# Larger first-stage and inverse units on three PSUM banks in a fused FFT filter and hardswish MLP

## The chip, the core and the metric

The kernel runs on one core of one Trainium2 chip. The metric is the device time of one launch in microseconds (us). The core's engines work side by side and each takes its own instructions in order: TensorE (PE: matmuls; PEld: its weight loads), VectorE (DVE), ScalarE (ACT), GpSimd (POOL) and SyncE (SP), whose queue here only issues DMAs.

## The reference

Eight sequences of 3008 rows and 256 columns are filtered along the rows in the frequency domain. The result, 24064 rows, goes through an MLP with a hardswish.

```python
X = np.fft.rfft(x, axis=1)                 # x: (8, 3008, 256)
Y = X * (filt_r + 1j * filt_i)[None]       # filter: (1505, 256)
y = np.fft.irfft(Y, n=3008, axis=1)
x = y.reshape(8 * 3008, 256)
h = x @ w_in                               # (256, 2048)
g = h * np.clip(h + 3.0, 0.0, 6.0) / 6.0
out = g @ w_out                            # (2048, 256)
```

All is in float32. A matmul in float32 leaves two records in the profile, one for each of its two passes.

## The kernel before

**The transform.** A sequence ("image" in what follows) has 3008 = 47 x 64 rows. The transform over the 47 is the first stage, the one over the 64 the second, and the inverse goes back the same way:

- The first stage works on 32 pairs of columns (HC). `a_unit(b, c)` (L439) takes four of them, in eight matmuls of 47 rows of contraction, 64 output rows and 256 columns. The contraction uses half of the array's rows and the output half of its columns, so four matmuls can be in the array at a time. The two halves h of the rows write into two PSUM banks from the pool psF, which has two buffers. ScalarE copies the first bank into the tile t1 (L449). `a_sums` (L453) lets VectorE subtract and add the second (L459, L460). `z_store` (L462) writes the four parts of the tile to the DRAM tensor z_tmp, by DMAs on POOL's queue.
- `x_load(b, c)` (L381) loads four pairs of columns into one of three buffers of the tile xs, with four DMAs on SP's queue. `t2_load` reads z_tmp back for the second stage.
- `b_unit` (L485) is the second stage, two y tiles at a time for images 2 to 7. `f_unit` (L505) multiplies with the filter on VectorE (L514 to L516), reading PSUM. `y_unit` (L519) combines the products into a y tile (L525, L526).
- `bi_unit(b, i)` (L530) is the first inverse stage: two y tiles, four matmuls of 64 rows, 64 output rows and 512 columns into two banks of psF. ScalarE copies both banks (L540) into the tile t3, of which there is one buffer (T3B). `g_store` (L550) writes it to g_tmp by DMAs on POOL's queue.
- `t4_load`, `n_unit` (L633) and `n_five` (L618) do the last inverse stage into the ring xn. Once a block of the ring is full, POOL forms the sums that the MLP needs (`t_sums`, L676, L683).

**The MLP.** There are 47 blocks of 512 rows (block 0 is done in a plain way). Each has eight steps p, one for each 256 of the 2048 hidden columns. Both products are done by Strassen's scheme, with seven smaller products in place of eight. One step on TensorE:

1. `up_1` (L689): A11 into the bank al, S1 and A12 into the bank be.
2. The place for early units, `do(0)`.
3. Down product 1 of the step before (L763).
4. `up_2` (L702): S2 into al, S4 into be. Afterwards VectorE reads be in `up_2b` (L713), which gives the first half of h.
5. Down products 2 and 4; `up_3`: S3 into al, which VectorE reads in L718; down products 5 and 6.
6. `up_4` (L720): ScalarE's relu of the first half; then the place `do(1)`.
7. VectorE's `hswish(k, p, 0)` (L737); `up_5` (L724): A22 into al, whose result ScalarE copies and puts through relu.
8. Down products 7 and 3, then the place `do(2)`.

al and be are one bank each (pool psU, one buffer), and four banks (psO) collect the down products. [...]

VectorE begins the next step with `g_sums` (L740): `hswish(k, p, 1)` (L737) and three sums (L744, L745, L747), on which down products 2 to 7 rest. L713, L718 and `hswish(k, p, 0)` follow.

At the end of a block, in the step p = 0 of the next one, `out_2` (L829) follows `hswish(k, p, 0)` on VectorE, and `out_3` (L834) follows the last down products 7 and 3. In p = 1, `out_4` (L838, L839) comes before L713 and `out_5` (L843) before `hswish(k, p, 0)`.

**The order.** It is written out by hand (`manual_schedule`). The dictionary `plan` holds, for each step of the whole run, what is put at its three places. Units of TensorE are in EARLY (L893) and go to place 0. What is not in EARLY, as `a_sums`, `f_unit`, `y_unit` and the DMAs, goes to place 2; place 1 holds only `w_scale`, early in the run. `places(n)` (L1058) gives the steps for image n. It counts them from 8 x `first[n]`, the first step of the block with which the image begins. Steps are named by this distance here: step -48 is 48 before it and so a step p = 0. For images 2 to 7 first-stage units stand at -54, -52, -49, -47, -45, -43, -42 and -41, inverse units at -32, -26, -23, -16, -10 and -7. One image takes about 47 steps of the MLP, so the stages of the next image lie under the MLP of the one before.

Of the kernel before, what the change touches and what calls it, by code (L numbers as in the profile page):

```python
# [10 lines left out]
FP32 = mybir.dt.float32  # L11
I32 = mybir.dt.int32
AXT = mybir.ActivationFunctionType
ALU = mybir.AluOpType
# [13 lines left out]
NA = 47  # L28
NC = 64
KH = 24  # L30
X0, XR = 16, 112
NF = N // 2 + 1
P = 128
D = 256
# [3 lines left out]
HC = NC // 2  # L38
XC = 4
NB = HC // XC  # L40
TC = 4
NT = KH // TC
TB = 3
# [138 lines left out]
def kernel(  # L182
# [64 lines left out]
    st = {}  # L247
# [130 lines left out]
    G11, G3, G1, G2, G4, G12, G22 = range(7)  # L378


    def x_load(b, c):  # L381
        t = xs[:, (b * NB + c) % 3, :, :]
        rows = x[b].rearrange("(a c) d -> a c d", c=NC)
        for h in range(2):
            for r, n in ((0, 32), (32, NA - 32)):
                nc.sync.dma_start(t[h * 64 + r:h * 64 + r + n, :, :], rows[r:r + n, ds(h * HC + c * XC, XC), :])

# [65 lines left out]
    def a_sums(b, c):  # L453
        t, ps = st["t1", b, c]
        if b == 1:
            if c >= NB - 2:
                nc.vector.tensor_copy(out=t[:, :, 1, :], in_=ps)
            return
        nc.vector.tensor_tensor(out=t[:, :, 1, :], in0=t[:, :, 0, :], in1=ps, op=ALU.subtract)  # L459
        nc.vector.tensor_tensor(out=t[:, :, 0, :], in0=t[:, :, 0, :], in1=ps, op=ALU.add)  # L460

    def z_store(b, c, q=nc.gpsimd):  # L462
        t = st.pop(("t1", b, c))[0]
# [66 lines left out]
    def bi_unit(b, i, ps=None):  # L530
        ys = [st.pop(("y", b, i + v)) for v in range(2)]
        ps = ps or [psF.tile([P, 2, D], FP32, name="psf", tag="f") for ri in range(2)]
        for v, ri in ((0, 0), (1, 0), (0, 1), (1, 1)):

            products = isinstance(ys[v], tuple)
            w, y = (wi[:, 1 + ri, :], ys[v][ri]) if products else (wi[ts(ri, 64), 0 if b else 3, :], ys[v][ts(ri, 64)])
            nc.tensor.matmul(ps[ri][ts(v, 64)], w, y, start=True, stop=True)  # L537
        t = (t3p if b or i & 2 else t1p).tile([P, 2, 2, D], FP32, name="t3" if b or i & 2 else "t1")
        for ri in range(2):
            nc.scalar.activation(out=t[:, ri, :, :], in_=ps[ri], func=AXT.Copy)  # L540
        st["t3", b, i] = t

    def g0_first(i):
        t = st["t3", 0, i]
# [348 lines left out]
    EARLY = (a_unit, b_unit, bi_unit, n_unit, n_five)  # L893

    def at(step, fn, *a):
        plan.setdefault((step, 0 if fn in EARLY else 1 if fn == w_scale else 2), []).append((fn, a))

    with tc.manual_schedule():

# [155 lines left out]

        def places(n):  # L1058
            if n == 1:
                return (list(range(2, NB + 2)), [12, 13, 15, 18, 19, 20, 22, 23, 26, 27, 28, 30],  # L1060
                        [14, 15, 16, 19, 21, 22, 24, 25, 27, 29, 30, 31], [16, 21, 24, 29, 31, 32])
            k = first[n] * NP
            a_at = [k - 7 * NP + i for i in (2, 4, 7, 9, 11, 13, 14, 15)]
            f_at, y_at, bi_at = ([k - (5 - 2 * r) * NP + i for r in range(2) for i in p]
                                 for p in ((2, 3, 6, 7, 12, 13), (4, 5, 10, 11, 14, 15), (8, 14, 17)))
            return a_at, f_at, y_at, bi_at

        at(n_at[TAIL - 2] + 1, lambda: nc.sync.dma_start(edge, wai_d[:, ds(NW + ND, ND)]))
# [2 lines left out]
        for n in range(1, B):  # L1071
            a_at, f_at, y_at, bi_at = places(n)
            for c, s in enumerate(a_at):
                at(s, a_unit, n, c)
                at(s, a_sums, n, c)
                at(s, z_store, n, c, nc.sync if n == 1 else nc.gpsimd)
                if c >= 3:
                    at(max(a_at[c - 3], s - 6), x_load, n, c)
                elif n > 1:
                    at(max(prev[c + NB - 3], s - 6), x_load, n, c)  # L1080
            for c in range(NT):
                s = f_at[2 * (c - TB) + (n == 1)] + 1 if c >= TB else a_at[-1] + 1
                at(s, t2_load, n, c)
                s = f_at[2 * (c - FB) + 1] + 1 if c >= FB else a_at[-1 if n > 1 else 3] + 1
                at(s, table_load, n, c)
            for i in range(NU):
                if i % 2 == 0 or n == 1:
                    at(f_at[i], b_unit, n, i)
                if i % 2 == 0:
                    at(bi_at[i // 2], bi_unit, n, i)  # L1090
                    at(bi_at[i // 2], g_store, n, i)
                at(y_at[i], y_unit, n, i)
            for i in range(NU):
                at(f_at[i], f_unit, n, i)
            prev = a_at
# [4 lines left out]
        for i in range(len(items) + 1):  # L1100
            up = i < len(items)
            k, p = items[min(i, len(items) - 1)]
            dn = i > 0
            kd, pd = items[i - 1]
            def do(place):
                for fn, a in plan.get((i, place), ()):
                    fn(*a)

            if k == 0:
                plain_up(p)  # L1110
                do(0)
# [12 lines left out]
            dn = dn and kd > 0  # L1124
            if dn:
                g_sums(kd, pd)
                down(kd, pd, 1)
            if up:
                up_2(k, p)
            if dn and pd == 0 and kd > 1:  # L1130
                out_4(kd - 1)
            if up:
                up_2b(k, p)
            if dn:
                down(kd, pd, 2, 4)
                if pd == NP - 1:
                    out_1(kd)
            if up:
                up_3(k, p)
            if dn:  # L1140
                down(kd, pd, 5, 6)
            if up:
                up_4(k, p)
                do(1)
            if ends:
                out_1(k)
            if last_plain:
                plain_down(pd, (0,))
            if dn and pd == 0 and kd > 1:
                out_5(kd - 1)  # L1150
            if up:
                hswish(k, p, 0)
            if up:
                up_5(k, p)
            if last_plain:
                plain_down(pd, (1,))
                plain_out()
            if dn:
                if pd == NP - 1 or ends:
# [35 lines left out]
```

## Time and profile before

| what | value |
|---|---|
| time, median of 3 runs | 2660.61 us (2660.59 to 2660.66) |
| the profiled execution | 2658.29 us |
| its span, first to last instruction | 2656.3 us |
| granted TensorE clock | 1.000 |
| first-stage matmuls L446, 896 records | 61.7 us busy, 389 ns mean |
| inverse matmuls L537 from y, 336 records | 51.2 us busy, 615 ns mean |
| ACT copy of a bank, 128x512, L449 | 600 ns mean |
| VectorE sums, 128x512, L459 and L460 | 681 and 687 ns mean |
| POOL's z stores L467, issue | 504 ns mean |
| POOL's g stores L553, issue | 591 ns mean |

The busy time of a row is the union of its instructions' times, so matmuls that run side by side count once. The mean is that of one record. In a timeline, each line has the start in us from the span's start, the time that the merged instructions took, engine, line, operation, what is written and read, shape and count.

### The profile page before, as it was taken

Reading aid. Unit: us, or ns where it says so; the run is one execution under the profiler, and the core shown is the slowest. Engines: PE = TensorE matmul, PEld = TensorE weight load, DVE = VectorE, ACT = ScalarE, POOL = GpSimd, SP = SyncE. Lnnn points to the kernel's source line nnn. Section 1 sums busy time; section 2 is a strip of 40 time slices with the busy share of each in tenths; the row PEclk is TensorE's granted clock in tenths of the full one; section 3 lists DMA queues with packets and bytes.
Section 4 is the critical chain, followed back from the end, with each engine's and each line's share of the span. In section 5 each row is a group of like instructions: output and inputs, shape, how many; then the busy total and the mean of one; then the engine's idle time right before and its main releaser. Section 6 shows DMA issues by size and latency. Waiting matters only on the chain.

```text
span 2656.3 us, 54240 instructions
## 1 busy us (share of the span) xinstructions
PE 2640.7 (99%) x21584; PEld 2316.5 (87%) x21584; DVE 2053.4 (77%) x3488; ACT 1318.7 (50%) x2688; POOL 495.6 (19%) x731
## 2 busy tenths in 40 slices
PE   9999999999999999999999999999999999999999
PEld 6688888888888888888888888888888888899998
DVE  7878868887688877888768887788877878766666
ACT  4554454555545554454544545545455454554554
POOL 2242021110311103111031210311113120111110
PEclk9999999999999999999999999999999999999999
DMA  9732233112241122411323113231122421110000
GB/s 251 216 91 74 68 96 105 56 36 81 79 109 56 36 83 76 109 56 37 87 72 109 56 40 85 70 109 56 49 77 70 109 59 50 42 43 21 20 20 24
DMA packets 134818, 198.24 MB, mean 75 GB/s; under 512 B 23146, under 2 KB 99016, under 8 KB 134374
## 3 DMA queue, kind: packets, MB, share of 16 engines
q1 hardware_dynamic: 117037, 150.12, 19.8%
q0 software_dynamic: 16960, 44.16, 6.3%
q8 instruction: 170, 2.79, 0.4%
q14 instruction: 82, 0.67, 0.1%
q10 hardware_dynamic: 569, 0.50, 0.1%
HBM read 122.43 MB, written 83.98 MB: 78 GB/s over the span
## 4 chain that ended last, share of the span: by engine, by line
PE 95%; DVE 2%; DMA 1%; issue 0%; ACT 0%; SPq 0%; POOL 0%; POOLq 0%; DVEq 0%; ACTq 0%
PE po L763 43%; PE al L687 24%; PE be L687 17%; PE psf L446 2%; PE psn L627 2%; PE psf L537 2%; PE psf L493 1%; PE po L806 1%; PE al L795 0%; PE be L795 0%; DMA w_all<-in_x_dram 0%; DVE g L737 0%; PE po L502 0%; DMA out_dram<-o 0%; PE psn L638 0%
## 5 line engine op out<-in xcount | busy, mean ns | idle before, releaser
L763 PEld LDWEIGHTS po<-w_all,g 128*128 128x128 f32 x10276 | 1362.1, 191 | 153.3 <-issue 44.5
L763 PE MATMUL po<-w_all,g 128*128 128x128 f32 x10276 | 1402.3, 276 | 0.1
L732 ACT ACTIVATE r<-h,half_c 128x512 f32<-128x512 f32 x736 | 532.9, 724 | 356.4 <-DVE h L713 344.5
L737 DVE SCALAR_TENSOR_TENSOR g<-r,h 128x512 f32<-128x512 f32 x736 | 531.3, 722 | 215.2 <-ACT r L732 203.2
L687 PE MATMUL al<-xt,w_all 128*128 128x256 f32 x2208 | 659.6, 381 | 0.1
L687 PE MATMUL be<-xt,w_all 128*128 128x256 f32 x1472 | 437.8, 379 | 0.0
L713 DVE TENSOR_TENSOR h<-be,s 128x512 f32<-128x512 f32 x368 | 253.8, 690 | 157.2 <-PE be L687 151.3
L687 PEld LDWEIGHTS al<-xt,w_all 128*128 128x128 f32 x2208 | 335.4, 192 | 1.0 <-issue 0.5
L687 PEld LDWEIGHTS be<-xt,w_all 128*128 128x128 f32 x1472 | 279.7, 190 | 37.9
L727 ACT ACTIVATE h<-al 128x256 f32<-128x256 f32 x368 | 141.7, 385 | 319.8 <-PE al L687 319.7
L718 DVE TENSOR_TENSOR h<-al,s 128x256 f32<-128x256 f32 x368 | 155.9, 424 | 149.6 <-PE al L687 148.5
L745 DVE TENSOR_TENSOR g<-g 128x512 f32<-128x512 f32 x367 | 261.7, 713 | 12.6
L708 ACT ACTIVATE s<-al 128x256 f32<-128x256 f32 x368 | 141.8, 385 | 194.6 <-PE al L687 191.2
L553 POOL DMA_DIRECT2D g_tmp<-t x96 | 55.4, 591 | 938.2 <-ACT t L540 926.2
L699 ACT ACTIVATE s<-be 128x256 f32<-128x256 f32 x368 | 141.7, 385 | 175.9 <-PE be L687 175.9
L687 PE MATMUL al<-xn,w_all 128*128 128x256 f32 x736 | 222.5, 384 | 1.4 <-DVE h L718 1.3
L687 PE MATMUL be<-xn,w_all 128*128 128x256 f32 x736 | 218.9, 379 | 0.0
L683 POOL TENSOR_TENSOR xt<-xn 128x256 f32<-128x256 f32 x184 | 136.7, 761 | 433.7 <-ACT xn L609 399.6
L744 DVE TENSOR_TENSOR g<-g 128x256 f32<-128x256 f32 x367 | 172.7, 471 | 12.5
L698 ACT ACTIVATE s<-al 128x256 f32<-128x256 f32 x368 | 141.8, 385 | 67.8 <-PE al L687 67.8
L747 DVE TENSOR_TENSOR g<-g 128x256 f32<-128x256 f32 x367 | 160.1, 436 | 12.5
L467 POOL DMA_DIRECT2D z_tmp<-t x192 | 95.3, 504 | 364.9 <-DVE t L460 347.5
(152 smaller groups left out, 1846.7 us busy)
## 6 DMA issues: line engine op xcount, KB each, us to landing
g_tmp<-t POOLq DMA_DIRECT2D x96, 256.0 KB, 3.7
t<-g_tmp SPq DMA_DIRECT2D x184, 120.0 KB
t<-z_tmp SPq DMA_DIRECT2D x42, 512.0 KB
z_tmp<-t POOLq DMA_DIRECT2D x192, 96.0 KB, 2.5
xs<-in_x_dram SPq DMA_DIRECT2D x112, 128.0 KB
o_tmp<-o SPq DMA_DIRECT2D x46, 256.0 KB
ft<-in_filt_r_dram SPq DMA_DIRECT2D x168, 64.0 KB
ft<-in_filt_i_dram SPq DMA_DIRECT2D x168, 64.0 KB
```

What stands on the lines that cost most here:

```text
L687: nc.tensor.matmul(ps, w_in[p][:, w, :], x, start=start, stop=stop, skip_group_check=True)
L698: nc.scalar.activation(out=s[:, 0, :], in_=al, func=AXT.Copy)
L699: nc.scalar.activation(out=s5, in_=be[:, 1, :], func=AXT.Copy)
L708: nc.scalar.activation(out=s[:, 1, :], in_=al, func=AXT.Copy)
L713: nc.vector.tensor_tensor(out=st["h"][0].rearrange("p (a n) -> p a n", a=2), in0=be, in1=s, op=ALU.add)
L718: nc.vector.tensor_tensor(out=st["h"][1][:, 256:512], in0=al, in1=s5, op=ALU.add)
L732: nc.scalar.activation(out=r, in_=st["h"][i], func=AXT.Relu, bias=half_c, scale=1.0 / 6.0)
L737: nc.vector.scalar_tensor_tensor(out=st["g", k, p][:, o:o + 2, :].rearrange("p a n -> p (a n)"), in0=st["r", i], scalar=1.0, in1=st["h"][i ...
L744: v.tensor_tensor(out=g[:, G1, :], in0=g[:, G3, :], in1=g[:, G22, :], op=ALU.add)
L745: v.tensor_tensor(out=g[:, G3:G2 + 1:2, :], in0=g[:, G3:G1 + 1, :], in1=g[:, G11:G11 + 1, :].broadcast_to([P, 2, 256]), op=ALU.subtract)
L747: v.tensor_tensor(out=g[:, G4, :], in0=g[:, G12, :], in1=g[:, G2, :], op=ALU.subtract)
L763: nc.tensor.matmul(st["po", k][bank][:, part, u, :], g[:, a, ts(u, P)], w_out[p][:, w, :], start=(p == 0 and n in OPENS and u == 0), stop= ...
```

## The change

The change touches images 2 to 7; image 1 keeps its units.

- `a6_unit`, `a6_sums` and `z6_store` take the place of `a_unit`, `a_sums` and `z_store`. A unit has six pairs of columns in 12 matmuls, three rounds of four. Per image there are five of these and one of two pairs of columns (SIX). The third bank is be, the one that `up_1` and `up_2` use. In round 1 the half h = 1 writes into be, in round 3 the half h = 0. ScalarE copies 64 columns of be after round 1 and the other 192 at the end.
- `bi3_unit` and `g3_store` take the place of `bi_unit` and `g_store`: three y tiles, again 12 matmuls of 256 columns on two banks of psF and on be. VectorE copies be in two parts, ScalarE one bank in the unit and the other in `bi3_copies`, after `up_5`.
- Both units go to place 1, between `up_4` and `up_5`, so just ahead of A22.
- The tile t3 gets three parts and serves both kinds of unit; there is still one buffer. xs serves as two buffers of six pairs of columns.
- First-stage units now stand at -52, -50, -48, -46, -43 and -41, inverse units at -30, -23, -14 and -7. The y units move from (4, 5, 10, 11, 14, 15) to (4, 5, 8, 10, 14, 15) in each half of the image, so from -30 and -29 to -32 and -30, and from -14 and -13 to -16 and -14.

```diff
+SIX = tuple(range(0, HC, 6))
...
+    def x_at(b, c):
+        if b == 1:
+            return xs[:, (b * NB + c) % 3, :, :], c * XC, XC
+        t = xs.rearrange("p i j d -> p (i j) d")
+        return t[:, ds((b * len(SIX) + c) % 2 * 6, 6), :], SIX[c], min(6, HC - SIX[c])
+
     def x_load(b, c):
-        t = xs[:, (b * NB + c) % 3, :, :]
+        t, c0, n_ = x_at(b, c)
...
+    def a6_unit(b, c):
+        xc, c0, n = x_at(b, c)
+        n //= 2
+        t = t3p.tile([P, 3, 2, D], FP32, name="t3")
+        banks = [psF.tile([P, 512], FP32, name="psf", tag="f") for h in range(2)]
+        be = psU.tile([P, 512], FP32, name="be") if n == 3 else None
+        for r in range(n):
+            for g in range(2):
+                for h in range(2):
+                    j, ps, o = (2, be, h) if r == 2 - 2 * h and n == 3 else (r - h if n == 3 else 0,) + (banks[h], r - h if n == 3 else 0)
+                    q = g * n + j
+                    nc.tensor.matmul(ps[ts(g, 64), ts(o, D)], wa[ds(h * 64, NA), ds((c0 + q) * 2 * KH, 64)],
+                                     xc[ds(h * 64, NA), q, :], start=True, stop=True)
+            if n == 3 and r == 0:
+                nc.scalar.activation(out=t[:, 2, 1, 0:64], in_=be[:, D:D + 64], func=AXT.Copy)
+        m = min(n, 2)
+        two = [ps[:, 0:m * D].rearrange("p (j d) -> p j d", d=D) for ps in banks]
+        nc.scalar.activation(out=t[:, 0:m, 0, :], in_=two[0], func=AXT.Copy)
+        if n == 3:
+                nc.scalar.activation(out=t[:, 2, 1, 64:D], in_=be[:, D + 64:], func=AXT.Copy)
+        st["t1", b, c] = t, be, two[1], n
+
+    def a6_sums(b, c):
+        t, be, ps, n = st["t1", b, c]
+        v, m = nc.vector, min(n, 2)
+        if n == 3:
+            v.tensor_tensor(out=t[:, 2, 0, :], in0=be[:, 0:D], in1=t[:, 2, 1, :], op=ALU.add)
+            v.tensor_tensor(out=t[:, 2, 1, :], in0=be[:, 0:D], in1=t[:, 2, 1, :], op=ALU.subtract)
+        v.tensor_tensor(out=t[:, 0:m, 1, :], in0=t[:, 0:m, 0, :], in1=ps, op=ALU.subtract)
+        v.tensor_tensor(out=t[:, 0:m, 0, :], in0=t[:, 0:m, 0, :], in1=ps, op=ALU.add)
...
+    def bi3_unit(b, i):
+        ys = [st.pop(("y", b, i + v)) for v in range(3)]
+        c = psU.tile([P, 512], FP32, name="be")
+        banks = [psF.tile([P, 512], FP32, name="psf", tag="f") for ri in range(2)]
+        t = t3p.tile([P, 3, 2, D], FP32, name="t3")
+        to = [t[:, q, :, :].rearrange("p u d -> p (u d)") for q in range(3)]
+        for r in range(3):
+            for v in range(2):
+                for ri in range(2):
+                    x, u, ps, o = (2, v, c, ri) if r == 2 * ri else (v, r - 1 + ri, banks[ri], r - 1 + ri)
+                    nc.tensor.matmul(ps[ts(v, 64), ts(o, D)], wi[ts(ri, 64), 0, :], ys[x][ts(ri, 64), u, :], start=True, stop=True)
+            if r == 0:
+                nc.vector.tensor_copy(out=to[2][:, 0:64], in_=c[:, 0:64])
+        nc.scalar.activation(out=to[1], in_=banks[1], func=AXT.Copy)
+        nc.vector.tensor_copy(out=to[2][:, 64:512], in_=c[:, 64:512])
+        st["t3", b, i] = t
+        st["bi3"] = to[0], banks[0]
+
+    def bi3_copies():
+        if "bi3" in st:
+            to, ps = st.pop("bi3")
+            nc.scalar.activation(out=to, in_=ps, func=AXT.Copy)
...
     def at(step, fn, *a):
-        plan.setdefault((step, 0 if fn in EARLY else 1 if fn == w_scale else 2), []).append((fn, a))
+        plan.setdefault((step, 0 if fn in EARLY else 1 if fn in (w_scale, bi3_unit, a6_unit) else 2), []).append((fn, a))
...
+        A_AT = (4, 6, 8, 10, 13, 15)
...
-            a_at = [k - 7 * NP + i for i in (2, 4, 7, 9, 11, 13, 14, 15)]
+            a_at = [k - 7 * NP + i for i in A_AT]
             f_at, y_at, bi_at = ([k - (5 - 2 * r) * NP + i for r in range(2) for i in p]
-                                 for p in ((2, 3, 6, 7, 12, 13), (4, 5, 10, 11, 14, 15), (8, 14, 17)))
+                                 for p in ((2, 3, 6, 7, 12, 13), (4, 5, 8, 10, 14, 15), (10, 17)))
...
             if up:
                 up_5(k, p)
+            bi3_copies()
```

`z6_store` and `g3_store` issue four DMAs for each unit on POOL's queue, as `z_store` did; `g_store` issued two.

More of the change, by code (lines that the diff above doesn't have):

```diff
@@ L385, in x_load @@
             for r, n in ((0, 32), (32, NA - 32)):
-                nc.sync.dma_start(t[h * 64 + r:h * 64 + r + n, :, :], rows[r:r + n, ds(h * HC + c * XC, XC), :])
+                nc.sync.dma_start(t[h * 64 + r:h * 64 + r + n, 0:n_, :], rows[r:r + n, ds(h * HC + c0, n_), :])
     def x0_at(o, n):
@@ L460, in a_sums, with z6_store @@
         nc.vector.tensor_tensor(out=t[:, :, 0, :], in0=t[:, :, 0, :], in1=ps, op=ALU.add)
+    def a6_unit(b, c):
[27 more added lines that the diff above has]
+        v.tensor_tensor(out=t[:, 0:m, 0, :], in0=t[:, 0:m, 0, :], in1=ps, op=ALU.add)
+    def z6_store(b, c):
+        t, _, _, n = st.pop(("t1", b, c))
+        for g in range(2):
+            for ri in range(2):
+                p0 = g * 64 + ri * KH
+                nc.gpsimd.dma_start(z_d[b, :, ri, ds(SIX[c] + n * g, n), :, :].rearrange("k j s d -> k (j s d)"),
+                                    t[p0:p0 + KH, 0:n, :, :].rearrange("p j s d -> p (j s d)"))
     def z_store(b, c, q=nc.gpsimd):
@@ L537, in bi_unit @@
             nc.tensor.matmul(ps[ri][ts(v, 64)], w, y, start=True, stop=True)
-        t = (t3p if b or i & 2 else t1p).tile([P, 2, 2, D], FP32, name="t3" if b or i & 2 else "t1")
+        t = t3p.tile([P, 3, 2, D], FP32, name="t3")[:, 0:2] if b or i & 2 else t1p.tile([P, 2, 2, D], FP32, name="t1")
         for ri in range(2):
@@ L541, in bi_unit, with g3_store @@
         st["t3", b, i] = t
+    def bi3_unit(b, i):
[6 more added lines that the diff above has]
+            for v in range(2):
+                for ri in range(2):
+                    x, u, ps, o = (2, v, c, ri) if r == 2 * ri else (v, r - 1 + ri, banks[ri], r - 1 + ri)
[10 more added lines that the diff above has]
+            nc.scalar.activation(out=to, in_=ps, func=AXT.Copy)
+    def g3_store(b, i):
+        t = st.pop(("t3", b, i))
+        for v in range(2):
+            nc.gpsimd.dma_start(g_d[b, :, :, ds(2 * (i + v), 2), :].rearrange("c ri u d -> c ri (u d)"),
+                                t[ts(v, 64), 0:2].rearrange("p ri u d -> p ri (u d)"))
+        for u in range(2):
+            nc.gpsimd.dma_start(g_d[b, :, :, 2 * (i + 2) + u, :], t[ts(u, 64), 2])
     def g0_first(i):
@@ L1073 @@
             for c, s in enumerate(a_at):
[L1074 to L1078, printed above, removed]
+                at(s, a_unit if n == 1 else a6_unit, n, c)
+                at(s, a_sums if n == 1 else a6_sums, n, c)
+                at(s, *((z_store, n, c, nc.sync) if n == 1 else (z6_store, n, c)))
+                if c >= (3 if n == 1 else 2):
+                    at(max(a_at[c - 3 + (n > 1)], s - 6), x_load, n, c)
                 elif n > 1:
-                    at(max(prev[c + NB - 3], s - 6), x_load, n, c)
+                    at(max(prev[-1 if n == 2 else c - 2], s - 6), x_load, n, c)
             for c in range(NT):
@@ L1088 @@
                     at(f_at[i], b_unit, n, i)
-                if i % 2 == 0:
+                if n == 1 and i % 2 == 0:
                     at(bi_at[i // 2], bi_unit, n, i)
                     at(bi_at[i // 2], g_store, n, i)
+                if n > 1 and i % 3 == 0:
+                    at(bi_at[i // 3], bi3_unit, n, i)
+                    at(bi_at[i // 3], g3_store, n, i)
                 at(y_at[i], y_unit, n, i)
```

## The prediction, made before the changed kernel was run

> **What bounds the kernel now.** I read the busy shares and the chain of waits first (page, parts 1 and 4), then TensorE's timeline in one stage of one image, then VectorE's in the same stretch.
>
> ```profile
> PE 2640.7 (99%) x21584; PEld 2316.5 (87%) x21584; DVE 2053.4 (77%) x3488; ACT 1318.7 (50%) x2688; POOL 495.6 (19%) x731
> ...
> PE 95%; DVE 2%; DMA 1%; issue 0%; ACT 0%; SPq 0%; POOL 0%; POOLq 0%; DVEq 0%; ACTq 0%
> ```
>
> TensorE ends 95% of the chain: the time is the sum of its steps plus its stalls. A busy PE hides stalls, so I take the length of each step, from one A11 product (first al of a step) to the next. TensorE's timeline, start and duration in us:
>
> ```profile
> 706.00 0.60 PE L687 MATMUL al<-xt,w_all 128*128 128x256 f32 x2
> ...
> 712.15 0.60 PE L687 MATMUL al<-xt,w_all 128*128 128x256 f32 x2
> ...
> 713.01 0.59 PE L687 MATMUL be<-xt,w_all 128*128 128x256 f32 x2
> 713.54 1.09 PE L446 MATMUL psf<-xs,wa 47*64 47x256 f32 x16
> 714.56 0.71 PE L763 MATMUL po<-w_all,g 128*128 128x128 f32 x4
> ...
> 719.52 0.60 PE L687 MATMUL al<-xt,w_all 128*128 128x256 f32 x2
> ```
>
> A bare step is 6.15 (706.00 to 712.15), one with a first-stage unit 7.37: the unit costs 1.22. A pass of 256 columns is issued every 0.216 us (713.01 to 713.44 for two), and 16 records on four array tiles are four such passes, 0.87. The other 0.35 is paid once per unit: 0.09 before it, 0.05 in its first pass, 0.11 behind it and 0.10 in the next product. An inverse unit costs 1.22 too. So fewer, longer units save 0.35 for each one dropped. VectorE over the start of a block (about 698.63), where no stall is seen:
>
> ```profile
> 698.09 0.68 DVE L829 TENSOR_TENSOR o<-po,p 128x512 f32<-128x512 f32 x1
> 698.88 0.42 DVE L834 TENSOR_TENSOR o<-po,o 128x256 f32<-128x256 f32 x1
> 699.22 0.68 DVE L737 SCALAR_TENSOR_TENSOR g<-r,h 128x512 f32<-128x512 f32 x1
> ...
> 701.47 0.41 DVE L838 TENSOR_TENSOR o<-po,o 128x256 f32<-128x256 f32 x1
> 701.80 0.41 DVE L839 TENSOR_TENSOR o<-po,o 128x256 f32<-128x256 f32 x1
> ...
> 705.25 0.68 DVE L459 TENSOR_TENSOR t<-t,psf 128x512 f32<-128x512 f32 x1
> 705.97 0.69 DVE L460 TENSOR_TENSOR t<-t,psf 128x512 f32<-128x512 f32 x1
> ```
>
> out_3 (L834) starts 0.25 into the step p=1, 0.09 after the last down product of the block ends (697.74+1.05): it waits for it. out_4 (L838, L839) then adds 0.7 before the next h (L713). This step has an early unit, which covers that. A bare step where VectorE is late (start 776.60):
>
> ```profile
> 778.07 0.69 DVE L737 SCALAR_TENSOR_TENSOR g<-r,h 128x512 f32<-128x512 f32 x1
> ...
> 780.44 0.69 DVE L713 TENSOR_TENSOR h<-be,s 128x512 f32<-128x512 f32 x1
> 781.05 0.41 DVE L718 TENSOR_TENSOR h<-al,s 128x256 f32<-128x256 f32 x1
> ```
>
> hswish(1) starts 1.47 into the step, L718 ends 3.39 later, and A22, which writes the same bank, is late: the next A11 is at 782.94, the step 6.34, a stall of 0.19. Other late bare steps agree: length = end of L718 + 1.48, and nothing is lost while hswish(1) starts before about 1.27. That is VectorE's deadline.
>
> **What the Trainium skill says.** "TensorEngine Tiling (Array Packing)", Key Properties: changing the tiling mode drains TensorE. The trace agrees: 0.35 per unit. Its PSUM Bottleneck section says that tiling speeds TensorE up, not the evacuation; what follows turns on that. "TensorE: Matmul & The Clock Gate", engine queue depths: ScalarE and VectorE are strict FIFO; here L834 stands still for a down product with later work behind it. "SBUF — State Buffer", shared port pair: VectorE with two SBUF inputs and GpSimd block each other; at 819.17 an L744 beside an L683 took 0.84 in place of 0.42.
>
> **The change part by part**, for one of the six images (2 to 7); steps are counted from its first block, so step -48 is 48 before it.
>
> 1. First-stage units. Before 8 x 1.22 = 9.76. After, five of three rounds (1.22+0.43 = 1.65) and one of a single round (1.22-0.43 = 0.79): 9.05, a gain of 0.71. But round 3 writes into be, which an ACT copy of 64 columns reads after round 1, so TensorE waits for it. With the unit starting at 4.91 (A22's usual 4.82 plus 0.09), round 1 ends at 5.58, the copy runs 5.63 to 5.85 (0.23, on the line through 0.385 for 256 and 0.60 for 512 columns), and round 3, due at 5.83, starts at 5.90 and pays its first-pass 0.05 again: 0.12. The trace has no such wait; bounds 0 and 0.25, I take 0.12. Gain left 0.71 - 0.60 = 0.11.
>
> 2. Inverse units. Before 6 x 1.22 = 7.30, after 4 x 1.65 and the same wait, now on a VectorE copy of 64 columns (0.22 by the same kind of line): 7.08. Gain 0.22.
>
> 3. Cover moved. At -32, -26, -16 and -10 an early inverse unit waited 0.09 for banks that the products with the filter still held, four times 0.09 = 0.36, now gone. But those steps are bare now, with hswish(1) at 1.47, so each loses 0.19 as the one shown: 0.77. Net loss 0.41. Against it, the stalls at -30 and -14 (0.15 and 0.26, VectorE beside GpSimd) vanish behind the units put there: gain 0.41.
>
> 4. The sums. A unit's be part needs ACT's third copy: two banks' copy 6.05 to 6.65, last 192 columns to 7.02. VectorE finishes hswish(0) at 5.7 and stands idle until 7.05; then two sums of 0.42 (be free at 7.94) and two of 0.69 to about 9.2. The step is now 6.15+1.65+0.12 = 7.92. S1, due at 0.43 of the next step (8.35), is not held. hswish(1) starts 1.26 to 1.43 into it: at the deadline, a stall of 0 to 0.15. Four such steps (-51, -49, -45, -42, all bare) at 0.05: 0.2. y sums moved to -32 make VectorE late in -31; 0.05 there and in -15: 0.1.
>
> 5. The third unit stands at -48, the step p=0. There VectorE's order is hswish(0), out_2, out_3, sums. out_3 waits for the block's last down product, which the unit has pushed back: 7.92+0.25 = 8.17 to 8.59. The be sums run 8.5 to 9.40, so S1 of step -47, due at 8.35, waits until 9.44, 1.1 us. Behind it stand all further products. Then the two larger sums end at 10.7, hswish(1) starts at 10.63 (overlap 0.08), and this is step p=1, with out_4: L718 ends 3.39+0.70 later, 14.72, which is 6.80 into the step; its length is 8.28 against 6.15 for a bare one. Loss 2.13. Before, no first-stage unit stood in a step p=0.
>
> 6. Costed at nothing: POOL issues 24 z stores and 16 g stores in place of 32 and 12, 21.5 us in place of 23.2 by their 504 and 591 ns (part 5 of the page and its rows L467, L553), and SP 24 x loads in place of 32; x loads of six columns are queued on SP two units ahead, over 27 us; z stores leave POOL's queue about 15 us after the unit's step starts, the next unit needs the single t3 buffer at about 20; ACT's late inverse copy ends at 8.9 and A11's copy by 9.34, just before S2's weights are wanted at 9.38. If any cover is gone the price is the excess itself; for the store I would expect none below 5 us of delay. The first image keeps its units; the last steps have none.
>
> Sum per image: -0.11 - 0.22 + 0.41 - 0.41 + 0.3 + 2.13 = +2.1, six images +12.6. The profiled execution took 2658.3 (span 2656.3 and 2.0 around it), so 2670.9; the median shown is 2.3 above it: 2673.2.
>
> **The rivals.**
> - Waits for the 64-column copies are hidden: 9 units x 0.12 x 6 = 6.5 less, 2666.7. For it: 0.07 of the 0.12 is weight loading that may run ahead. Against: the wait stands on the first product of round 3, and its weights too are held.
> - Sums late everywhere: without the overlap and with slower copies hswish(1) starts at 1.6 and four steps per image lose 0.3 more: +7, 2680. For it: VectorE idles in front of the sums, so every delay of ACT passes on. Against: ACT has nothing else queued there.
> - The switch is cheap at its new place: between down products and A22 the 0.35 may shrink, since another shape stands before and behind. At most 54 units x 0.35 = 19 saved, 2654; the sign turns from 0.23 per unit on. Against: no such discount is seen at any unit of the trace, and a late A22 pays the same 0.10 in its first product.
> - out_3 waits for product 7 only, or the sums are not held: point 5 falls to about 1.7 or, unheld, 0.1; the latter gives 2661. Against: both products share the bank that L834 reads, and it starts 0.09 after the second.
>
> **How the numbers follow.** Main course 0.50, copies hidden 0.20, sums late 0.14, cheap switch 0.09, no hold at the block start 0.07 (half of it with the copies hidden too, below 2656). The likeliest time is 2673. The range runs from 2664 (copies hidden and 1.7 at point 5) to 2681. The measurement tells about 0.2% (5 us) from no change. Faster: 0.09 and a third of the last case, 0.11; same: 0.06; slower: 0.83.
>
> **What would show it.** Right: step -47 of each of the six images some 2 us longer than a bare one, S1 waiting for VectorE there; unit steps near 7.9; bare steps at -32, -26, -16, -10 of 6.34. Wrong: -47 near 6.2, or unit steps near 7.5. The prediction falls if no product waits for a sum out of be.

## The result, and the profile after

| | before | after |
|---|---|---|
| time, median | 2660.64 us (2660.59 to 2661.08, 4 runs) | 2692.58 us (2691.71 to 2693.0, 4 runs) |
| the profiled execution | 2658.29 us | 2691.71 us |
| its span | 2656.3 us | 2689.7 us |

The changed kernel is slower: the ratio is 1.0119, with a 95% interval of 1.0102 to 1.0137. The two profiled executions differ by 33.4 us. The prediction was 2673 us, 12.4 above the median before, so its sign holds and its size does not; 2692.58 lies above its range.

The page after, its busy time and the shares of the chain of waits:

```profile
PE 2652.5 (99%) x21872; PEld 2336.9 (87%) x21872; DVE 2072.1 (77%) x3572; ACT 1309.2 (49%) x2712; POOL 487.1 (18%) x707
...
PE 87%; DVE 9%; issue 2%; ACT 1%; DMA 1%; POOL 0%; DVEq 0%; POOLq 0%; SPq 0%; ACTq 0%
```

PE is still "99% busy", so that number shows nothing of the loss. The chain does: VectorE's share rose from 2% to 9%, TensorE's fell from 95% to 87%. The view of waits names them. TensorE's rows after (engine, what is written, line, the work waited for: us in total, times, longest):

```profile
PE po L840 <- DVE o L916: 6.5, 22, 0.7
PE be L764 <- DVE t L496: 5.8, 6, 1.0
PE po L840 <- DVE o L920: 5.3, 12, 0.4
PE al L764 <- DVE h L795: 4.5, 8, 1.5
```

L840 is a down product, L764 a product of `up_1` to `up_5`, L496 the second sum out of be, L795 the second half of h; L906, L911, L916 and L920 are `out_2` to `out_5`; L814 is the hswish, L790 and L795 are what L713 and L718 were. The second row was foreseen. The first and the third were not, and in the kernel before neither of them reaches 0.5 us. The fourth stood at 1.3 before; nearly all that is new in it are two waits of 1.49, at -13 of images 6 and 7, which were not foreseen either. These are idle times of TensorE alone, 22 us in all, and not the whole loss: a late product can cost its step more than the idle time ahead of it (below, an idle time of 0.44 goes with a step longer by 0.71).

I therefore set every step's length (first A11 product to the next) against the same step before, and added up the six images:

| steps | what changed | us, six images | predicted |
|---|---|---|---|
| those with first-stage units | five units of 1.79 and one of 0.79 for eight of 1.22 | -0.1 | -0.7 |
| -47 | the be sums hold S1 | +11.4 | +12.8 |
| -32, -26, -16, -10 | 7.455 to 6.345, no unit any more | -26.6 | the three rows of inverse units together: -1.3 |
| -30, -14 | 6.30 and 6.40 (image 3) to 7.92, a unit | +19.3 | |
| -23, -7, the larger unit alone | 7.365 to 7.92 | +6.7 | |
| -23, -7, beyond 7.92 | `out_5` and `out_4` are late | +10.9 | 0 |
| -31, -15 | y sums behind `out_3` | +7.7 | +0.6 |
| -29, -13 | VectorE is late, 3.5 us of it beside GpSimd | +4.2 | 0 |
| -51, -49, -45, -42 | follow a unit | 0.0 | +1.2 |

The sum, before rounding, is +33.5 (with 0.1 of step -27), and the executions differ by 33.4; what lies outside these steps adds nothing on balance. The three rows above the last, 22.8 us, are what the prediction lacked, but for 0.6. Each in turn.

**Step -47, as predicted.** Timelines after, image 3; the step starts at 705.60. TensorE:

```profile
705.60 0.60 PE L764 MATMUL al<-xt,w_all 128*128 128x256 f32 x2
707.16 0.67 PE L764 MATMUL be<-xn,w_all 128*128 128x256 f32 x2 [0.96 <-DVE t L496]
...
711.29 1.16 PE L840 MATMUL po<-w_all,g 128*128 128x128 f32 x8 [0.40 <-DVE o L916]
...
713.65 0.60 PE L764 MATMUL al<-xt,w_all 128*128 128x256 f32 x2
```

VectorE in the same stretch:

```profile
705.80 0.42 DVE L911 TENSOR_TENSOR o<-po,o 128x256 f32<-128x256 f32 x1 [1.85 <-PE po L840]
706.14 0.41 DVE L495 TENSOR_TENSOR t<-be,t 128x256 f32<-128x256 f32 x1
706.59 0.42 DVE L496 TENSOR_TENSOR t<-be,t 128x256 f32<-128x256 f32 x1
...
708.24 0.69 DVE L814 SCALAR_TENSOR_TENSOR g<-r,h 128x512 f32<-128x512 f32 x1
...
710.83 0.41 DVE L916 TENSOR_TENSOR o<-po,o 128x256 f32<-128x256 f32 x1
```

`out_3` (L911) stood still for 1.85 us for the last down product, with the be sums behind it. L496 ends at 707.01, and S1 starts at 707.16 in place of 706.03. The step is 8.05, where a bare one takes 6.15. TensorE's third line shows something else that was not foreseen: down product 5 waits for `out_4` (L916).

**Steps -23 and -7: what stands behind the unit's copies.** TensorE after, step -7 of image 3 (starts at 981.47):

```profile
986.39 0.43 PE L599 MATMUL be<-y,wi 64*64 64x256 f32 x1
...
989.10 1.16 PE L840 MATMUL po<-w_all,g 128*128 128x128 f32 x8 [0.44 <-DVE o L920]
990.10 0.60 PE L764 MATMUL al<-xt,w_all 128*128 128x256 f32 x2
```

VectorE:

```profile
985.60 0.42 DVE L795 TENSOR_TENSOR h<-al,s 128x256 f32<-128x256 f32 x1
987.10 0.23 DVE L601 COPY t<-be 128x64 f32<-128x64 f32 x1 [1.07 <-PE be L599]
988.09 0.62 DVE L603 COPY t<-be 128x448 f32<-128x448 f32 x1 [0.77 <-PE be L599]
988.63 0.41 DVE L920 TENSOR_TENSOR o<-po,o 128x256 f32<-128x256 f32 x1
```

In the kernel before, in the same step (starts at 972.76), `out_5` (L843) follows the second half of h at once:

```profile
978.11 0.42 DVE L718 TENSOR_TENSOR h<-al,s 128x256 f32<-128x256 f32 x1 [0.56 <-PE al L687]
978.45 0.41 DVE L843 TENSOR_TENSOR o<-po,o 128x256 f32<-128x256 f32 x1
```

L601 and L603 are the unit's own copies of be. They wait 1.07 and 0.77 for TensorE, and `out_5` (L920), which had nothing to wait for since 986.0, stands behind them until 988.63. `out_5` is the last reader of the bank that down product 7 of the new block opens. So product 7 starts at 989.10, 0.06 after `out_5` ends. The Trainium skill ("TensorE: Matmul & The Clock Gate", engine queue depths) calls VectorE a strict FIFO; here this costs 0.71 in each of twelve steps. In -23 of five images product 5 waits as well, for `out_4`, here in image 3 (the step starts at 872.04):

```profile
876.36 1.16 PE L840 MATMUL po<-w_all,g 128*128 128x128 f32 x8 [0.23 <-DVE o L916]
```

Those steps are longer by another 0.49, 9.11 in all.

**Steps -31 and -15: the y sums behind `out_3`.** VectorE after, step -31 of image 3 (starts at 816.09):

```profile
816.46 0.42 DVE L911 TENSOR_TENSOR o<-po,o 128x256 f32<-128x256 f32 x1
816.90 0.69 DVE L571 TENSOR_TENSOR y<-s 64x512 f32<-64x512 f32 x1
817.62 0.69 DVE L572 TENSOR_TENSOR y<-s 64x512 f32<-64x512 f32 x1
818.41 0.69 DVE L814 SCALAR_TENSOR_TENSOR g<-r,h 128x512 f32<-128x512 f32 x1
...
821.41 0.41 DVE L916 TENSOR_TENSOR o<-po,o 128x256 f32<-128x256 f32 x1
```

In the kernel before, the same step (starts at 810.06) has no sums between `out_3` and hswish(1), which starts 0.59 into it:

```profile
810.31 0.42 DVE L834 TENSOR_TENSOR o<-po,o 128x256 f32<-128x256 f32 x1
810.65 0.68 DVE L737 SCALAR_TENSOR_TENSOR g<-r,h 128x512 f32<-128x512 f32 x1
```

The y unit belongs to step -32, a step p = 0. What `do(2)` issues there comes after `out_3`, and `out_3` waits for the last down product. So the y sums run inside the next step, and hswish(1) starts 2.32 into it where the prediction put the deadline at 1.27. The step before had no unit to give it room. Loss: 0.49 in nine steps, where an `n_unit` early in the step covers some of it, 0.08 in -31 of image 7, and 1.59 in -15 of images 6 and 7, where none stands.

**Steps -29 and -13.** 3.5 of the 4.2 us are two steps, -13 of images 6 and 7. The rest are nine steps by 0.07 each, in which hswish(1) starts at 1.47, after the deadline. VectorE, GpSimd and TensorE after, -13 of image 6 (starts at 1950.78):

```profile
1952.97 0.43 DVE L821 TENSOR_TENSOR g<-g 128x256 f32<-128x256 f32 x1
1953.08 1.24 POOL L618 DMA_DIRECT2D g_tmp<-t  x2
...
1953.43 0.69 DVE L822 TENSOR_TENSOR g<-g 128x512 f32<-128x512 f32 x1
1954.16 2.55 DVE L824 TENSOR_TENSOR g<-g 128x256 f32<-128x256 f32 x1
1954.16 2.26 POOL L760 TENSOR_TENSOR xt<-xn 128x256 f32<-128x256 f32 x3
...
1957.70 0.70 PE L764 MATMUL al<-xn,w_all 128*128 128x256 f32 x2 [1.49 <-DVE h L795]
```

L821, an instruction of the same size, takes 0.43. L824 takes 2.55, and ends 0.29 after three GpSimd sums that began at the same moment. The Trainium skill ("SBUF — State Buffer", shared port pair) says that VectorE with two SBUF inputs and a GpSimd instruction that reads SBUF shut each other out for a whole instruction. The trace fits this, and here the delay runs over three instructions in a row. A22 (L764) then waits 1.49 for L795, the second half of h. On GpSimd's queue the three sums stand directly behind the store issues of the unit at -14 (L618 is the last of them), so they begin together 3.4 into the step. In the kernel before that step has no store, and its first two sums begin 2.2 into it.

### The profile page after: what moved, and what is told of

The parts are those of the page before. It is cut to its first block, busy times and chain, and to the rows that moved or that the text cites. A ratio compares the mean times of both kernels' runs of the same rounds, so it can differ in the third digit from the quotient of the medians.

```text
span 2689.7 us, 54858 instructions
## 1 busy us (share of the span) xinstructions
PE 2652.5 (99%) x21872; PEld 2336.9 (87%) x21872; DVE 2072.1 (77%) x3572; ACT 1309.2 (49%) x2712; POOL 487.1 (18%) x707
## 4 chain that ended last, share of the span: by engine, by line
PE 87%; DVE 9%; issue 2%; ACT 1%; DMA 1%; POOL 0%; DVEq 0%; POOLq 0%; SPq 0%; ACTq 0%
PE po L840 39%; PE al L764 21%; PE be L764 16%; PE psn L704 2%; DVE g L814 2%; PE psf L539 1%; PE psf L480 1%; DVE g L822 1%; PE po L883 1%; DVE h L790 1%; DVE g L821 1%; ACT r L809 1%; PE be L599 1%; PE psf L599 1%; PE be L480 1%
## 5 line engine op out<-in xcount | busy, mean ns | idle before, releaser
L840 PEld LDWEIGHTS po<-w_all,g 128*128 128x128 f32 x10276 | 1365.3, 191 | 135.7 <-DVE g L821 16.8
L840 PE MATMUL po<-w_all,g 128*128 128x128 f32 x10276 | 1397.2, 276 | 12.6 <-DVE o L916 6.5
L814 DVE SCALAR_TENSOR_TENSOR g<-r,h 128x512 f32<-128x512 f32 x736 | 528.1, 717 | 241.3 <-ACT r L809 227.2
L764 PE MATMUL al<-xt,w_all 128*128 128x256 f32 x2208 | 659.7, 381 | 0.1
L764 PE MATMUL be<-xt,w_all 128*128 128x256 f32 x1472 | 437.8, 379 | 0.0
L764 PEld LDWEIGHTS al<-xt,w_all 128*128 128x128 f32 x2208 | 335.4, 192 | 1.0 <-issue 0.5
L790 DVE TENSOR_TENSOR h<-be,s 128x512 f32<-128x512 f32 x368 | 253.2, 688 | 104.7 <-PE be L764 95.5
L764 PEld LDWEIGHTS be<-xt,w_all 128*128 128x128 f32 x1472 | 279.7, 190 | 37.9
L822 DVE TENSOR_TENSOR g<-g 128x512 f32<-128x512 f32 x367 | 261.8, 713 | 12.6
L764 PE MATMUL al<-xn,w_all 128*128 128x256 f32 x736 | 231.7, 397 | 4.5 <-DVE h L795 4.5
L795 DVE TENSOR_TENSOR h<-al,s 128x256 f32<-128x256 f32 x368 | 155.1, 422 | 94.7 <-PE al L764 92.9
L764 PE MATMUL be<-xn,w_all 128*128 128x256 f32 x736 | 219.4, 380 | 5.8 <-DVE t L496 5.8
L821 DVE TENSOR_TENSOR g<-g 128x256 f32<-128x256 f32 x367 | 170.7, 465 | 12.6
L824 DVE TENSOR_TENSOR g<-g 128x256 f32<-128x256 f32 x367 | 166.0, 452 | 12.5
L764 PEld LDWEIGHTS be<-xn,w_all 128*128 128x128 f32 x736 | 139.3, 190 | 26.6 <-PE al L764 8.0
L917 POOL TENSOR_TENSOR o<-p,o 128x256 f32<-128x256 f32 x46 | 36.8, 800 | 589.1 <-DVE o L915 541.1
```

The costliest lines, as they stand in the source:

```text
L764: nc.tensor.matmul(ps, w_in[p][:, w, :], x, start=start, stop=stop, skip_group_check=True)
L790: nc.vector.tensor_tensor(out=st["h"][0].rearrange("p (a n) -> p a n", a=2), in0=be, in1=s, op=ALU.add)
L795: nc.vector.tensor_tensor(out=st["h"][1][:, 256:512], in0=al, in1=s5, op=ALU.add)
L814: nc.vector.scalar_tensor_tensor(out=st["g", k, p][:, o:o + 2, :].rearrange("p a n -> p (a n)"), in0=st["r", i], scalar=1.0, in1=st["h"][i ...
L821: v.tensor_tensor(out=g[:, G1, :], in0=g[:, G3, :], in1=g[:, G22, :], op=ALU.add)
L822: v.tensor_tensor(out=g[:, G3:G2 + 1:2, :], in0=g[:, G3:G1 + 1, :], in1=g[:, G11:G11 + 1, :].broadcast_to([P, 2, 256]), op=ALU.subtract)
```

## The experiments

Each is compared with the kernel before; "after" is the changed kernel.

**1. The third unit one step later, and the fourth with it.** Theory: of the 33 us, 11 come from one unit in a step p = 0. Rival: the sums after any unit cost as much.

```diff
-        A_AT = (4, 6, 8, 10, 13, 15)
+        A_AT = (4, 6, 9, 11, 13, 15)
```

> The third and fourth first-stage units of images 2 to 7 stand one step later (-47 and -45 in place of -48 and -46), so none stands in a step p = 0. Theory, point 5 of the prediction: the sums of the unit at -48 stand behind out_3 on VectorE and hold S1 and then A22 of step -47, which takes 8.05 us where a bare step takes 6.15. Without it the six images lose 1.90 less each: 11.4 us less than the changed kernel, about 2681, and no product waits for a sum out of be. Rival: the single t3 buffer or the store behind it holds the unit wherever it stands; then the loss moves to the step after -47 or to the next unit, and the time stays within 3 us of 2692.

Measured: 2680.96 us (2679.84 to 2681.37), ratio 1.0078 (1.0061 to 1.0095); 11.6 below after, 11.1 by the steps. TensorE's waits in this kernel:

```profile
PE po L840 <- DVE o L920: 5.3, 12, 0.4
PE al L764 <- DVE h L795: 4.5, 8, 1.5
PE po L840 <- DVE o L916: 4.1, 16, 0.7
```

The row of L496 is gone, and six of L916 with it, those of step -47. Step -47 with a unit now takes 7.94, and the bare step after it 6.15. Point 5 of the prediction is thus shown, and with it that a unit elsewhere costs the step after it next to nothing (0.03 in -44, none in the others).

**2. `out_5` ahead of the unit.** Only the order on VectorE changes. Theory: the queue behind the copies makes product 7 late. Rival: the longer unit itself does.

```diff
             if up:
                 up_4(k, p)
+            if dn and pd == 0 and kd > 1:
+                out_5(kd - 1)
+            if up:
                 do(1)
...
-            if dn and pd == 0 and kd > 1:
-                out_5(kd - 1)
```

> out_5 stands ahead of the inverse unit's copies on VectorE, nothing else moves. Theory: in step p = 1 the down products of the new block's last bank wait for out_5, and out_5 stands behind the copies of be out of the unit, which end only after the unit. That is 0.71 us in each of the twelve steps -23 and -7. Moved, these steps lose 0.71 less each: 8.5 us less than the changed kernel, about 2684; about 0.49 us stays in the five steps -23 where out_4 is late beside GpSimd. Rival: the inverse unit itself is slower in these steps, for y tiles or the t3 buffer; then steps -23 and -7 keep 9.1 and 8.6 us and the time stays within 2 us of 2692.

Measured: 2683.71 us (2683.32 to 2684.8), ratio 1.0091 (1.0076 to 1.0106); 8.9 below after, 8.4 by the steps. VectorE in step -7 of image 3 (starts at 979.20):

```profile
983.34 0.42 DVE L795 TENSOR_TENSOR h<-al,s 128x256 f32<-128x256 f32 x1
983.68 0.41 DVE L920 TENSOR_TENSOR o<-po,o 128x256 f32<-128x256 f32 x1
984.83 0.23 DVE L601 COPY t<-be 128x64 f32<-128x64 f32 x1 [0.74 <-PE be L599]
985.83 0.62 DVE L603 COPY t<-be 128x448 f32<-128x448 f32 x1 [0.77 <-PE be L599]
```

`out_5` now runs in time in which VectorE only waited. Step -7 goes from 8.63 to 7.92, step -23 from 9.11 to 8.40, 0.71 each; the 0.49 by `out_4` stays. The unit and its copies are the same, so the rival falls.

**3. The third y unit one step later**, so out of the step p = 0.

```diff
-   ... (4, 5, 8, 10, 14, 15), (10, 17)))
+   ... (4, 5, 9, 10, 14, 15), (10, 17)))
```

> The third y unit of each half image stands one step later (-31 and -15 in place of -32 and -16). Theory: in the step p = 0 its 1.4 us come after out_2 and out_3 on VectorE, which was late already, and hold out_4 and A22 in -31 and -15: 0.49 us in ten steps with an early unit, 1.59 in two without. Without it 8 us less; in the step after, -30 or -14, the unit ahead of A22 covers VectorE. Some of it may come back there and in -29 and -13 (y beside GpSimd), up to 0.3 us in each of twelve: 4 us back. About 2685 to 2688. Rival: these steps are long for GpSimd's sums or the last inverse stage; then they keep 8.15 us and the time stays within 2 us of 2692.

Measured: 2692.52 us (2692.21 to 2693.88), ratio 1.0124 (1.0109 to 1.0139), as after. The expected gain came: -31 and -15 are back at what they took before the change, 7.7 us less. It was given back in the next steps: nine of the twelve at -30 and -14 rise from 7.92 to between 8.67 and 8.88 (+7.9 us), so the 2685 to 2688 that were expected did not come. The rival named the time, but not its reason: -31 and -15 did not keep their 8.15. VectorE, GpSimd and TensorE, step -30 of image 3 (starts at 825.36):

```profile
825.50 1.18 POOL L760 TENSOR_TENSOR xt<-xn 128x256 f32<-128x256 f32 x1
826.12 1.11 DVE L572 TENSOR_TENSOR y<-s 64x512 f32<-64x512 f32 x1
826.76 1.05 POOL L760 TENSOR_TENSOR xt<-xt 128x256 f32<-128x256 f32 x1
827.33 1.03 DVE L814 SCALAR_TENSOR_TENSOR g<-r,h 128x512 f32<-128x512 f32 x1
...
828.42 1.16 PE L840 MATMUL po<-w_all,g 128*128 128x128 f32 x8 [0.29 <-DVE g L814]
...
831.07 0.43 PE L599 MATMUL be<-y,wi 64*64 64x256 f32 x1 [0.17 <-DVE h L790]
```

The same two sums and the hswish take 1.11 and 1.03 in place of 0.69, each beside a GpSimd sum. Then the down products are late, and at the end the inverse unit itself waits for L790, because it writes into be, which L790 reads: a wait that a unit on two banks did not have. So the place of the y unit causes the loss at -31 and -15, but moving it by one step only moves the loss: beside an inverse unit at -30 or -14 VectorE is late at both places.

**4. The copy between the rounds, 8 columns for 64** (the later copies take 248 and 504). This copy orders the writes of the two halves into be. Without it they could be in the one bank at once, so it was made short and not taken out, which wasn't tried.

```diff
-  nc.scalar.activation(out=t[:, 2, 1, 0:64], in_=be[:, D:D + 64], func=AXT.Copy)
+  nc.scalar.activation(out=t[:, 2, 1, 0:8], in_=be[:, D:D + 8], func=AXT.Copy)
...
-  nc.vector.tensor_copy(out=to[2][:, 0:64], in_=c[:, 0:64])
+  nc.vector.tensor_copy(out=to[2][:, 0:8], in_=c[:, 0:8])
```

> The copy after round 1, which separates the two row halves' writes into be, has 8 columns in place of 64; the second copy has the other 248 or 504. Theory, points 1 and 2 of the prediction: round 3 waits for this copy, so each unit is shorter by what the copy is, some 0.045 us on ScalarE and 0.06 on VectorE: steps of first-stage units 7.90 in place of 7.94, of inverse units 7.86 in place of 7.92, in all 2.5 to 3 us less than the changed kernel. Rival: the units' cost over three rounds is the switch of the array's tiling alone; then the unit steps keep their length, and the time is the same or longer, since the second copies are longer.

Measured: 2689.6 us (2687.57 to 2690.23), ratio 1.0111 (1.0096 to 1.0126); 3.0 below after, 3.7 by the steps. The copy's line in after (count, then shortest, median and longest ns):

```profile
L483 ACT ACTIVATE t<-be x30: 224/224/225, 338.3 to 2085.3; 128x64 f32<-128x64 f32 x30
```

and in this kernel:

```profile
L483 ACT ACTIVATE t<-be x30: 177/178/178, 339.7 to 2084.3; 128x8 f32<-128x8 f32 x30
```

An eighth of the columns saves 47 ns, and the unit steps fall by the same, from 7.942 to 7.895: whatever the copy gets shorter, the unit gets shorter, so TensorE waits for the copy's end. That is 1.4 us over 30 units. At -30 and -14 the inverse units fall by 57 ns, 0.7 us in all; at -23 and -7 nothing changes, since product 7 still waits there for `out_5`. The rest is not so clean: -29 and -13 rise by 0.06 nearly everywhere, while -13 of images 6 and 7 fall by 1.14 each. So the units' own share is 2.1, and 2.3 us are a collision with GpSimd that happened to shrink. That the sum falls within the expected 2.5 to 3 is luck.

**5 and 6. Each half of the change alone.** In the first only the first-stage units are new, in the second only the inverse units, with their y units.

```diff
-                 ... (4, 5, 8, 10, 14, 15), (10, 17)))
+                 ... (4, 5, 10, 11, 14, 15), (8, 14, 17)))
...
-                if n == 1 and i % 2 == 0:
+                if i % 2 == 0:
...
-                if n > 1 and i % 3 == 0:
+                if False:
```

> The first-stage units of six columns alone; the inverse units, y units and their places are those of the kernel before. Theory: the shorter TensorE work is eaten by the wait for the 64-column copy (five units of 1.79 and one of 0.79 against eight of 1.22: 0.02 us gained per image), and the step -47 loses 1.90: 6 x 1.88 = 11.3 us slower than before, about 2672. Rival: the two parts disturb each other through the single t3 buffer or be, and most of the 32 us is in their being together; then this one alone costs less than 5 us.

```diff
-        if b == 1:
+        if True:
...
-            a_at = [k - 7 * NP + i for i in A_AT]
+            a_at = [k - 7 * NP + i for i in (2, 4, 7, 9, 11, 13, 14, 15)]
...
-                at(s, a_unit if n == 1 else a6_unit, n, c)
+                at(s, a_unit, n, c)
...
```

> The inverse units of three y tiles alone, with their places and y places; first-stage units are those of the kernel before. Theory: what is not the first stage's, 33 - 11.3 = about 22 us slower than before, about 2682 (the 3.5 us of steps -13 of the last two images hang on GpSimd's timing and may be missing). Rival: as for the first stage alone, the cost is in their being together, and this one alone costs less than 10 us.

Measured, over the steps of the images: +11.5 and +22.2, together 33.7 against 33.5 of the whole change. The two halves do not act on each other. The medians are 2677.06 (2675.7 to 2678.8), ratio 1.0065 (1.005 to 1.008), and 2683.55 (2683.12 to 2684.36), ratio 1.0089 (1.0074 to 1.0104). The first is some 6 us above what its steps explain. They lie behind all the work: this is VectorE's last instruction in that kernel, whose span is 2673.9,

```profile
2662.10 0.69 DVE L859 TENSOR_TENSOR o<-psf,o 128x512 f32<-128x512 f32 x1 [0.24 <-PE psf L852]
```

and in the kernel before, whose span is 2656.3:

```profile
2650.49 0.69 DVE L782 TENSOR_TENSOR o<-psf,o 128x512 f32<-128x512 f32 x1 [0.24 <-PE psf L775]
```

The span ends 11.1 us after it there, and 5.2 us in the kernel before. TensorE has ended by then in both, so no step of it is longer. What the program waits for at its end is open; for this kernel I use the steps and not the median.

**7. The places mended.** Experiment 1 and 4, the y units of before, and inverse units at (11, 16), so at -29, -24, -13 and -8: two of them one step later, away from -30 and -14, and two ahead of `out_4` and `out_5`.

```diff
-   ... (4, 5, 8, 10, 14, 15), (10, 17)))
+   ... (4, 5, 10, 11, 14, 15), (11, 16)))
```

> Both kinds of larger unit, with places that keep them out of the way of the block's end: first-stage units at 4, 6, 9, 11, 13, 15; y units at their old places; inverse units at 11 and 16 in place of 10 and 17, so that none stands in a step p = 1; first copies of 8 columns. Theory: against the changed kernel 11.4 less for -47, 10.9 less for -23 and -7, 7.1 less for -31 and -15, about 3.5 less for -13 of two images, 3 less for the copies, 2.5 more where the y units beside GpSimd stand in bare steps -30 and -14 again: about 2659, even with the kernel before. Rival: larger units cost more by themselves, wherever they stand (PSUM bank be, t3); then it stays above 2668.

Measured: 2662.6 us (2661.49 to 2663.86, 12 runs), ratio 1.001 (1.0001 to 1.0018). 30 of the 33 us are gone, 3.6 fewer than expected. A unit in a step p = 0 leaves the step p = 1 after it bare, and that one holds `out_4`: -23 takes 6.74 (+0.59) in five images and 6.43 (+0.29) in the sixth, and -7 takes 6.43 in all six, where 6.15 was expected. That is 5.0 us, more than the miss.

**8. The filter products and y units spread out**, on top of 7, so that fewer steps have VectorE late.

```diff
-   ... (2, 3, 6, 7, 12, 13), (4, 5, 10, 11, 14, 15)
+   ... (2, 4, 6, 7, 12, 14) and (2, 3, 6, 7, 12, 14), (3, 5, 10, 11, 13, 15) and (4, 5, 10, 11, 13, 15)
```

(the first of each pair in the first half of an image, the second in the second)

> As the run with mended places, and the second filter product of three pairs per image stands two steps behind the first, with a y unit between them (first half: products 2, 4, 6, 7, 12, 14 and y 3, 5, 10, 11, 13, 15; second half: products 2, 3, 6, 7, 12, 14 and y 4, 5, 10, 11, 13, 15). Theory: two products in a row make VectorE late by 0.4 us and cost a bare step 0.19; three of these per image go: 3.4 us less than the run with mended places, about 2655, below the kernel before. Rival: the longer hold of psF's two banks or the later y units hold TensorE elsewhere; then it is not faster than the run with mended places.

Measured: 2659.16 us (2658.35 to 2660.56, 12 runs), ratio 0.9998 (0.9989 to 1.0007). The difference to 7 is the expected one, 3.4, from -36, -26 and -10 at 6.15 in place of 6.35; its level is off by the miss of 7.

**9. As 8, with the inverse units at (11, 17) and `out_5` ahead of their copies as in 2.** Against 8:

```diff
-   ... p[min(r, len(p) - 1)]
+   ... p[min(r, len(p) - 1, n < 6 and 0 or 1)]
...
-   ... ((11, 16),)
+   ... ((11, 17), (11, 17))
```

The first pair of lines was to give both halves the first half's places of the products in images 2 to 5. It does not: `n < 6 and 0 or 1` is 1 for every n, so these places are those of 8.

> As the run with products spread, but the inverse units stand at 11 and 17, with out_5 ahead of their copies on VectorE, and the first pair of each half has its products two steps apart (in images 6 and 7 in the first half alone). Theory: at 16 the unit costs 0.59 in five steps -23 and 0.29 in six steps -7 by the late out_4; at 17 behind out_5 there is no loss in -7, and the 0.49 of out_4 beside GpSimd stays in five steps -23. With 0.19 for each of four more spread pairs that is 2 to 3.5 us less than the run with products spread: about 2656.5, 0.1% below the kernel before. Rival: out_4 and out_5 are late at 17 as well, or y units in -21 hold something; then it stays at 2659 or above.

Measured: 2656.39 us (2655.16 to 2657.32, 21 runs), ratio 0.9988 (0.9981 to 0.9994): faster than before by 3.2 us. TensorE's waits for VectorE now:

```profile
PE al L764 <- DVE h L795: 1.3, 5, 0.5
...
PE po L840 <- DVE o L916: 1.0, 5, 0.2
```

Step -7 takes 7.86 and loses nothing. What is left is -23 of five images, 0.47 each. Part of the expected gain was to come from four more spread pairs, which this kernel does not have: step -20 still takes 6.34 in those images. What it gains over 8 lies at -24, -23, -8 and -7 (2.6 us by the steps).

**10. How much of that is the larger units?** The kernel before, its units as they were, with only the first pair of filter products in a half spread in the same way.

```diff
-   ... (2, 3, 6, 7, 12, 13), (4, 5, 10, 11, 14, 15), (8, 14, 17)
+   ... (2, 4, 6, 7, 12, 13), (3, 5, 10, 11, 14, 15), (8, 14, 17)
```

(the second half of images 6 and 7 stays)

> The kernel before with the first pair of filter products of each half image two steps apart (in images 6 and 7 in the first half alone), as far as its inverse units let them; its units keep their size. Theory: ten stalls of 0.19 go, 2 us less than before: about 2658. If so, of what the last version gains over the kernel before, the larger units bring what is left over. Rival: the spread is worth something only with larger units; then the time is that of before.

Measured: 2657.39 us (2656.86 to 2661.62, 13 runs), ratio 0.9994 (0.9985 to 1.0002). By its steps it gains 1.9 us: 1.2 at -36 and 0.8 at -20 of four images. Kernel 9 gains 2.5, of which it has the 1.2 at -36 in the same way, and nothing at -20. So half of kernel 9's gain needs no larger unit. The other 1.3 us is what the larger units bring once all their places are mended, as far as single profiled executions tell; the medians of 9 and 10 differ by 1.0, and the intervals of their ratios overlap.

## Why the prediction was right and wrong

The step that failed is the path of the inverse units at -23 and -7. Point 2 ends it at TensorE's wait for the first copy of be, and puts what stands behind the copies on VectorE at nothing; there 10.9 us were lost. Two more terms were too small: the y sums of point 4 (0.6 predicted, 7.7 measured), and VectorE at -29 and -13 (nothing, 4.2). These 22.2 us cover the whole miss of 20.8 (33.4 where 12.6 was predicted); the errors of the other terms are small beside them, and points 1 and 5 held.

1. **First-stage units: right.** A unit of three rounds was put at 1.77 and measures 1.79. Above the 1.65 of three rounds that is 0.14 (0.12 predicted). Experiment 4 shows that round 3 waits for the copy; how much of the 0.14 is that wait is not shown. The rivals of hidden copies and of a cheap switch fall with this: the unit steps are near 7.9, and the single round costs the 0.79 that was predicted (the cheap switch was also costed with 54 units, where 60 are placed). So the gain from fewer units is nil, a little less than the 0.11 per image of point 1.
2. **Inverse units: the core was right.** 7.92 was predicted and 7.92 measured at -30 and -14 (in ten of twelve; the other two, 8.37, hold one more small unit in both kernels), 6.34 and 6.345 at the four steps left bare. Without the losses listed above, the inverse units come to -0.7 us where -1.3 was predicted.
3. **Where the unit's copies stand: missed.** Point 6 ends with the copies of ACT. For VectorE's own copies, point 2 counts only the wait of TensorE for the first. It did not ask what VectorE does next. In p = 1 that is `out_5`, and a down product needs it. What stands ahead of the prediction says of the down products only that they rest on `g_sums`; that the first into each bank also rests on the `out` that last read it was left out. Cost: 0.71 x 12 = 8.5 us, shown by experiment 2, and 0.49 x 5 = 2.4 for `out_4`, which stays when `out_5` is moved. That the early unit of before covered this last one is argued from the timelines, and not shown alone.
4. **The y sums: the term of point 4 was mis-sized.** Two times 0.05 per image was taken; it was 0.49 in nine steps, 1.59 in two and 0.08 in one. The error is the start of hswish(1): `out_3` and two sums stand ahead of it at the turn of a block, so it starts at 2.32, while 0.05 is what point 4 takes for a start at 1.26 to 1.43. The working was at hand: point 5 follows the same `out_3` through the same turn of a block for the first-stage sums. Experiment 3 shows that moving them back does not give the time back.
5. **The third unit: right.** 2.13 was predicted for -47 and 1.90 measured, with S1 held for 0.96 by the line that was named; experiment 1 took away 11.6.
6. **The sums after the other units: 1.2 us predicted, 0 measured.** hswish(1) starts 1.17 to 1.20 into these steps, in time, where 1.26 to 1.43 was predicted.
7. **VectorE at -29 and -13** (4.2) was not counted. 3.5 of it is one collision in each of two steps, and each is 1.14 shorter in experiment 4, whose unit at -14 is 0.06 shorter. In the profile of before no sum of 256 columns in the six images' steps takes even 1 us. Point 6 put the store issues on GpSimd at nothing; that they push its three sums together is seen in the one timeline, and was not tested.

Of the rivals, "sums late everywhere" came nearest in size, for another reason: it put the delay on ACT's copies, while the lost time stands at the turns of blocks.

## What to carry to other kernels

- When work is moved on a busy engine, follow its evacuation into the queue that does it, and then every instruction behind that, to its reader. Do it once for each kind of step: here p = 0 and p = 1 carry the `out` sums that the others lack, and 30 of the 33 us were lost in steps p = 1.
- A unit of TensorE is also cover for late engines around it. One unit in place of two takes a cover away, and a unit that comes after the products it covered gives none; this is argued from the timelines, where the bare -23 and -7 of experiment 7 lose 0.59 and 0.29.
- Merging units to save their fixed cost needs the price of what joins the parts: per image the first stage saved 2 x 0.35 by two units fewer, and paid 5 x 0.14 for the copies between rounds.

## What the runs showed of the hardware

- A copy out of PSUM by ScalarE takes 0.178 us for 8 columns and 0.224 for 64: an eighth of the columns costs four fifths of the time, so a copy that only orders two writes costs at 8 columns most of what it costs at 64.
- VectorE's subtraction of 256 columns from SBUF took 2.55 us in place of 0.42, in two steps, beside three GpSimd sums in a row. Beside a single one, a sum of 512 columns took 1.11 in place of 0.69.
